# Work of a cycle's parameters and magnitude products moved between ScalarE, VectorE and GpSimd in a fused S4D and MLP-mixer kernel

## The chip, the cores and the metric

The kernel runs on one core of a Trainium2 chip. The time is that of the device in microseconds for one execution of the whole program; the profile gives one execution, with the busy intervals of each engine: PE (matmul, TensorE), PEld (its weight loads), DVE (VectorE), ACT (ScalarE), POOL (GpSimd) and SP (the queue from which most transfers are issued).

## What is computed

The input is one sequence of L = 2048 tokens and D = 448 channels. A vector c gives six modulation vectors by one matrix, w_mod. Two blocks follow, each behind a layer norm that is scaled and shifted:

```python
mod = (silu(c) @ w_mod).reshape(1, 6, 1, -1)
h = layernorm(x) * (1 + ca) + sa
x = x + ga * S4D(h)          # long convolution
h = layernorm(x) * (1 + cb) + sb
x = x + gb * MLP(layernorm(h))   # over the tokens, 2048 -> 1792 -> 2048, gelu

# S4D: the convolution's kernel, for each channel d and N = 256 complex terms n
dt = exp(log_dt);  A = -exp(log_A_real) + 1j * A_imag;  C = (C_real + 1j * C_imag) * dt
K[d, l] = 2 * Re(sum_n C[d, n] * exp(A[d, n] * dt[d] * l))       # l = 0 .. 2047
y = irfft(rfft(h, 4096) * rfft(K, 4096))[:2048] + h * D_skip
```

All is float32. The convolution is done by matmuls with tables of sines and cosines.

## The kernel before

The first half of the program makes K, the transforms of h and their product; the second, from about 366 us, is the layer norm and the two matmuls of the MLP with streamed weights.

**Steps and cycles.** K is made in 56 steps s; a step covers 16 channels' worth of terms (128 rows by 512 columns, twice). The power l is split into a small part and a large part, so that each step makes two factors, E and G, as magnitude times sine or cosine, and PE sums over n with 64 small matmuls (`st_kgen`). Steps go in cycles of 8. At a cycle's start `window(s)` takes the exponentials of all 8 steps in a row: PE makes the exponents (`st_exponents`), ACT the magnitudes (`st_exp`), and between them other work is slipped in for e = 0 to 7. Then come the 8 steps with sines (`st_phase` on PE, `st_step`), so that ACT changes its function table only twice or three times per cycle.

**A step.** ACT does two Abs (L651, L652) and four Sin (L653 to L656). GpSimd multiplies the two halves of G (L658, L659), VectorE the four quarters of E (L660, L661, then, behind `between()`, L663, L664). E needs m2 = magnitude times w, where w is a product of two columns; `st_mag2` (L637, L639) makes both on GpSimd. In cycle 0 the first two of these stand in the window at e = 4 and 5, the others in the steps, two steps ahead. There are three m2 buffers (`m2p`).

**Parameters.** Channels come in four sets of 128 rows (the last has 64, folded to 128 x 128). For set 0, `first_chain` computes at once what the exponent and phase matmuls need: log-magnitudes, phases, and the phase of C by an arctangent, each split into a high and a low part, which SP stores to DRAM (`pars`) and loads as `lex` and `lph`. For sets 1 to 3, `chain(q)` does the same as a Python generator that yields after each instruction. `more(n)` takes n steps of it and stops at "logs" (the chain waits until the window of its cycle does its logarithms and exponential on ACT in `logs`) and at "end". In the windows `WPACE[s // 8][e]` says how many steps are taken, in the sine steps `pace` (2 per step, in `between()`). `chain` starts with two Abs on ACT (L392, L393) and goes on with VectorE; only the splits (L382, L384) are on GpSimd, and only while `aside` is set, that is in the windows of cycles 1 to 3. Sets 1, 2 and 3 are due one after the other: set 1 must be in DRAM for step 16, set 2 for step 32, set 3 for step 48.

**Beside it.** `u_stats` (L500, L501, VectorE) takes the mean and variance of x, `u_norm` normalises it, `u_rows` (PE L531, VectorE L534) and `u_cols` (PE L563, then VectorE L570 or ACT L572) transform it, with transfers through DRAM between. `u_cols` needs a table s2 (`s2_load`, L548), loaded by SP four columns ahead. `modulation(k)` multiplies c by a 448 x 448 part of w_mod (PE L487); the parts 0 to 2 are loaded into `wm0` (`wm_load`, L323), a big tile that is used for yk only from step 8 on. The back of `wm0` holds the split parts of set 0 until SP has stored them. x is loaded in parts, four rows by SP and the rest by GpSimd's own queue (L298) at the start and behind steps 1 and 2.

**Order.** PE, ACT, VectorE and GpSimd run in the order in which the program writes their instructions; SP does so up to step 8, and is ordered by the scheduler after that. Each engine's queue is in order. A transfer is counted on one of eight completion slots in turn, and its issue waits for the transfer before it in that slot.

Of the kernel before, what the change touches and what calls it, by code (L numbers as in the profile page):

```python
# [11 lines left out]
F32 = mybir.dt.float32  # L12
F32R = mybir.dt.float32r
BF16 = mybir.dt.bfloat16
AF = mybir.ActivationFunctionType
# [205 lines left out]
def tile_adaln_s4d_mixer(ctx, tc, i, out):  # L221
# [20 lines left out]
    with ExitStack() as es:  # L242
# [24 lines left out]

        raws = {}

        def par_load(q, eng=nc.sync):  # L270
            n = min(P, D - P * q)
            raws[q] = {}
            for nm in ("A_C_real", "A_C_imag", "A_log_A_real", "A_A_imag"):
                raws[q][nm] = qp.tile([P, N], F32, tag=nm, name=nm, bufs=2)
                for k in range(P // n):
                    c = slice(k * (N * n // P), (k + 1) * (N * n // P))
                    eng.dma_start(raws[q][nm][n * k : n * k + n, 0 : N * n // P], i[nm][P * q : P * q + n, c])

        ldt_v = i["A_log_dt"]
        ldt0 = qp.tile([P, 1], F32, name="ldt0")  # L280
# [88 lines left out]
        def chain(q):  # L369


            n = min(P, D - P * q)
            f = N * n // P
            cr, ci, a, aim = (raws[q][nm][:, 0:f] for nm in ("A_C_real", "A_C_imag", "A_log_A_real", "A_A_imag"))
            xa, ya, s, t, u, ph, p64 = (
                qp.tile([P, N], F32, tag=nm, name=nm)[:, 0:f] for nm in ("xa", "ya", "s", "t", "u", "ph", "p64")
            )

            def split(src, places):
                hl = qp.tile([P, 2, N], F32R, tag="hl", name="hl", bufs=3)[:, :, 0:f]  # L380
                eng = G if aside else V
                eng.tensor_copy(hl[:, 0], src)  # L382
                yield
                eng.tensor_tensor(hl[:, 1], src, hl[:, 0].bitcast(F32), ALU.subtract)  # L384
                for k, v in places:
                    for m in range(P // n):
                        to = pars[q][v, k, 0:n, :, m * f : (m + 1) * f]
                        nc.sync.dma_start(to, hl[n * m : n * m + n].bitcast(F32))
                yield


            S.activation(xa, cr, AF.Abs, scale=0.5)  # L392
            S.activation(ya, ci, AF.Abs, scale=0.5)  # L393
            tt(s, xa, ya, ALU.add)
            yield
            tt(ya, ya, xa, ALU.subtract)
            yield
            ts(s, s, 2.0**-120, None, ALU.max)
            yield
            V.reciprocal(xa, s)  # L400
            yield
            tt(ya, ya, xa, ALU.mult)
            yield

            ts(t, s, 2.0**-40, 2.0**80, ALU.is_lt, ALU.mult)
            yield
            stt(s, t, 1.0, s, ALU.max, ALU.mult)
# [12 lines left out]
            yield from split(s, [(2, 1)])  # L420
            yield "exponents"

            ts(ph, aim, dt4[:, q : q + 1], None, ALU.mult)
            yield
            ts(u, ph, MAGIC, MAGIC, ALU.add, ALU.subtract)
            yield
            tt(ph, ph, u, ALU.subtract)
# [5 lines left out]
            tt(p64, ph, u, ALU.subtract)  # L433
# [17 lines left out]
            tt(xa, xa, u, ALU.subtract)  # L451
            yield
            yield from split(xa, [(2, 0)])
# [180 lines left out]
        def st_mag2(s):  # L634
            me = v32(mags[s][:, 0])
            w = wp.tile([P, GD], F32, tag="w", name="w")
            G.tensor_tensor(w[:, :, None], me[:, :, 31:32], me[:, :, 1:2], ALU.mult)  # L637
            m2 = m2p[s >= 32 and s % BATCH > 2].tile([P, GD, 32], F32, tag="m2", name="m2")
            G.tensor_tensor(m2, me, w[:, :, None].to_broadcast([P, GD, 32]), ALU.mult)  # L639
            m2s[s] = m2  # L640

# [177 lines left out]
        def first_chain():  # L819
# [19 lines left out]
            def direct(hl, tile, r, g):  # L839

                nc.sync.dma_start(tile[g][r : r + 32].bitcast(F32), hl[16 * g : 16 * g + 16])
# [8 lines left out]
            S.activation(dt[:, 0:1], ldt0, AF.Exp)  # L850

            S.activation(one, one, AF.Ln)
            par_load(1, nc.scalar)

            ts(sr, cr, 0.0, 0.5, ALU.is_ge, ALU.subtract)
            ts(si_, ci, 0.0, 0.5, ALU.is_ge, ALU.subtract)
# [8 lines left out]
            for g in range(4):  # L865
                direct(ha, lex, 0, g)
                if g < 3:
                    direct(ha, lex, 64, g)
            x_load(0, 4, G)
            S.activation(u, ya, AF.Square)  # L870
            S.activation(u, u, AF.Ln, bias=1.0)
# [38 lines left out]
            store(hc, (2, 0))  # L910

        first_chain()
        for g in (1, 2):
            load(g, False)
        x_load(4, 2)
# [48 lines left out]
        def window(s):  # L964
            if s:
                aside.append(True)
            angle()
            logs(s == 8)
            if s == 8:
                u_scale()  # L970
                u_norm(0)
                u_norm(1)

            if s == 8:
                modulation(0, 0, 1)
            if s == 0:
                st_exponents(s)
            for e in range(BATCH):
                st_exp(s + e)

                if e + 1 < BATCH:
                    st_exponents(s + e + 1)
                else:
                    st_phase(s)
                mellow()
                flush(dve)
                flush(act)
                if s == 8 and e == 0:
                    tt(mod[1], mod[1], mod[2], ALU.mult)
                if s < 32:  # L990
                    more(WPACE[s // 8][e])
                if s == 0 and e >= 4:
                    u_stats(e - 4)
                if s == 8 and e == 1:

                    G.tensor_tensor(mod[0], mod[0], mod[2], ALU.mult)
                if s and e < (2 if s <= 32 else 1):
                    st_kgen(s - (2 if s <= 32 else 1) + e)
                elif e == 5:
# [12 lines left out]

                if s >= 40 and e == 2:
                    piece(False)
                if s >= 40 and e == 4:
                    piece(pieces[0] < NP)
                if s == 0 and e in (4, 5):
                    st_mag2(e - 4)
                elif s and (e < 2 or s >= 32):
                    st_mag2(s + e)  # L1020
                if s == 8 and e == 0:
                    u_norm(e + 2)
                if s == 0 and e == 3:
                    for r in range(4):
                        dsk_copy(r)
            aside.clear()
            if s == 0:

                S.activation(one, one, AF.Sin)

        WPACE = [[1] * 8, [4, 4, 4, 4, 4, 4, 4, 1], [4, 4, 4, 4, 4, 4, 4, 1], [2] * 8]
        pace = [2] * 32
        tail = NHALF + 3
        for s in range(tail):
# [33 lines left out]
            else:  # L1070
# [6 lines left out]

                if s > 32 and s % BATCH:
                    st_kgen(s - 1)
                st_step(s, between)  # L1080
            flush(act)
            if s == NHALF:
# [3 lines left out]
            if s in (1, 2):  # L1086
                x_load(4 + 4 * s, 4, G)
            free = s > 7 and not st_s1(s % BATCH == BATCH - 1)
            if s + 2 < 32 and (s + 2) % BATCH > 1:
                st_mag2(s + 2)  # L1090

            if 3 < s < 8:
# [274 lines left out]
```

## Time and profile before

| | |
|---|---|
| three runs | 715.1, 719.54, 722.51 us; median 719.54 |
| the profiled execution | 720.75 us, its span 719.0 us |
| PE busy | 648.0 us, 90% of the span |
| DVE, ACT, POOL busy | 431.4, 453.1, 271.7 us |
| granted clock of PE, mean | 0.962 |
| transfers | 128.00 MB, 178 GB/s |

The stages of the first half lie thus in the profile: first exponentials 18.1 to 28.6 us, sines of cycle 0 to 65.4, exponentials of cycle 1 to 94.8, sines to 131.7, exponentials of cycle 2 to 153.6, sines to 187.3, exponentials of cycle 3 to 203.1, sines to 240.9, and three more cycles to about 366 us. A line of the groups gives line, engine, operation, output from input, count, then busy microseconds and mean nanoseconds, then idle time of the engine before them and what ended it. A line of the timeline or of the chain begins with the start and the duration in microseconds.

### The profile page before, as it was taken

The page shows a single profiled execution, that of the slowest core. Times are in us where ns is not written, and L with a number is a line of the kernel's source. Part 1 is how long each engine was busy: PE and PEld are TensorE (multiplying, and loading weights), DVE is VectorE, ACT ScalarE, POOL GpSimd, SP SyncE. Part 2 cuts the span into 40 slices and gives each one's busy share as a digit, 9 for nine tenths or more (in the row PEclk, how much of TensorE's full clock was granted, in tenths as well). Part 3 has the DMA queues.
Part 4 walks back from the last instruction along what each step waited for, and adds up shares of the span by engine and source line. Part 5 has one row for each costly group of instructions (what it writes and reads, how often), then busy time and mean ns, then how long its engine had stood idle before and what let it go on. Part 6 is the DMA issues. An engine that isn't in the chain of part 4 may idle for free.

```text
span 719.0 us, 18067 instructions
## 1 busy us (share of the span) xinstructions
PE 648.0 (90%) x7090; PEld 479.3 (67%) x7090; DVE 431.4 (60%) x821; ACT 453.1 (63%) x849; POOL 271.7 (38%) x341
## 2 busy tenths in 40 slices
PE   0777999879979879898999979999999999999997
PEld 0443444435535556575679936778999999999996
DVE  7668768758577567584855448778622263334441
ACT  4877487887986989999947649787522242222220
POOL 5395657548656866867745600000000000000000
PEclk9998758998999989999999999999999999999999
DMA  8494545556867656555459999984585436555540
GB/s 196 154 200 130 194 141 178 204 162 197 250 194 237 186 119 178 147 156 156 137 156 282 296 255 251 248 218 115 171 231 150 145 110 175 168 159 154 154 142 26
DMA packets 99395, 128.00 MB, mean 178 GB/s; under 512 B 13546, under 2 KB 80622, under 8 KB 99310
## 3 DMA queue, kind: packets, MB, share of 16 engines
q1 hardware_dynamic: 97726, 122.78, 60.3%
q0 software_dynamic: 1008, 3.54, 2.2%
q8 instruction: 56, 0.92, 0.6%
q10 hardware_dynamic: 576, 0.52, 0.3%
q14 instruction: 29, 0.24, 0.1%
HBM read 91.46 MB, written 34.87 MB: 176 GB/s over the span
## 4 chain that ended last, share of the span: by engine, by line
PE 65%; ACT 12%; DMA 9%; DVE 6%; issue 3%; POOL 3%; SPq 1%; DVEq 0%; ACTq 0%; POOLq 0%
PE acc L1191 6%; PE o L1333 6%; PE o L1335 6%; PE o L1334 6%; PE acc L1193 6%; PE acc L1192 6%; PE xe L610 6%; PE kg L685 4%; DMA wm<-in_w_mod_dram 4%; PE vv L794 3%; PE kx L778 3%; PE vv L795 3%; PE pu L563 2%; PE xg L610 2%; PE pm L487 2%
## 5 line engine op out<-in xcount | busy, mean ns | idle before, releaser
L206 ACT CAST whi<-w 128x896 fp32r<-128x896 f32 x64 | 59.8, 937 | 135.5 <-PE o L1334 84.8
L658 POOL TENSOR_TENSOR G<-mag,gs 128x512 f32<-128x512 f32 x56 | 72.0, 1286 | 69.3 <-ACT gs L654 69.1
L215 DVE TENSOR_TENSOR wlo<-w,whi 128x896 fp32r<-128x896 f32 x64 | 68.0, 1086 | 43.2 <-ACT whi L206 37.0
L1191 PE MATMUL acc<-h3h,whi 128*128 128x448 f32 x224 | 82.8, 370 | 0.8 <-ACT h3h L1242 0.8
L1192 PE MATMUL acc<-h3l,whi 128*128 128x448 f32 x224 | 80.9, 361 | 0.7 <-DVE h3l L1249 0.5
L1193 PE MATMUL acc<-h3h,wlo 128*128 128x448 f32 x224 | 81.3, 363 | 0.0
L1333 PE MATMUL o<-uh,whi 128*128 128x448 f32 x224 | 81.3, 363 | 0.0
L1335 PE MATMUL o<-uh,wlo 128*128 128x448 f32 x224 | 81.2, 362 | 0.0
L1334 PE MATMUL o<-ul,whi 128*128 128x448 f32 x224 | 80.6, 360 | 0.0
L610 PE MATMUL xg<-tab,lph 64*128 64x512 f32 x112 | 66.7, 597 | 12.6 <-DVE E L664 7.7
L685 PEld LDWEIGHTS kg<-E,G 128*32 128x32 f32 x3584 | 56.7, 115 | 31.1 <-issue 16.4
L610 PE MATMUL xe<-tab,lph 64*128 64x512 f32 x112 | 65.7, 592 | 9.3 <-ACT gs L655 7.6
L659 POOL TENSOR_TENSOR G<-mag,gs 128x512 f32<-128x512 f32 x56 | 71.8, 1282 | 0.0
L685 PE MATMUL kg<-E,G 128*32 128x64 f32 x3584 | 66.5, 229 | 3.4 <-ACT ks L699 2.0
L660 DVE TENSOR_TENSOR E<-m,xe 128x512 f32<-128x512 f32 x56 | 38.4, 686 | 46.6 <-ACT xe L653 30.3
L639 POOL TENSOR_TENSOR m<-mag,w 128x512 f32<-128x512 f32 x56 | 58.7, 1049 | 4.4
L1337 DVE SCALAR_TENSOR_TENSOR y<-o,b,mod 128x448 f32<-128x448 f32 x16 | 11.0, 685 | 80.2 <-PE o L1335 80.2
L1191 PEld LDWEIGHTS acc<-h3h,whi 128*128 128x128 f32 x224 | 42.0, 188 | 12.8 <-ACT h L1247 5.6
L786 DVE TENSOR_TENSOR z<-kx,u 128x448 f32<-128x448 f32 x48 | 28.4, 620 | 32.5 <-PE kx L778 32.5
L610 PE MATMUL xe<-tab,lex 64*128 64x512 f32 x56 | 29.8, 544 | 19.7 <-DMA lex<-wm 18.1
L651 ACT ACTIVATE ab<-xe 128x512 f32<-128x512 f32 x56 | 33.9, 606 | 17.4 <-PE xg L610 9.9
L1192 PEld LDWEIGHTS acc<-h3l,whi 128*128 128x128 f32 x224 | 41.9, 187 | 4.1 <-DVE h3l L1249 0.8
(221 smaller groups left out, 1514.7 us busy)
## 6 DMA issues: line engine op xcount, KB each, us to landing
w<-in_B_w_dram SPq DMA_DIRECT2D x64, 224.0 KB
w<-in_B_w_dram SPq DMA_DIRECT2D x32, 448.0 KB
u<-us_d SPq DMA_DIRECT2D x48, 224.0 KB
yu_d<-yt SPq DMA_DIRECT2D x16, 448.0 KB
yi<-yu_d SPq DMA_DIRECT2D x32, 224.0 KB
us_d<-uo SPq DMA_DIRECT2D x16, 448.0 KB
v_d<-vt SPq DMA_DIRECT2D x32, 224.0 KB
vt<-v_d SPq DMA_DIRECT2D x16, 448.0 KB
```

The lines of the kernel that those rows point to most:

```text
L206: self.nc.scalar.copy(hi, w)
L215: eng.tensor_tensor(lo, w, hi.bitcast(F32), ALU.subtract)
L610: T.matmul(out[k], lhs[r], rhs[r], start=start, stop=stop)
L658: G.tensor_tensor(Gt[:, 1], mg_, v32(sg), ALU.mult)
L659: G.tensor_tensor(Gt[:, 0], mg_, v32(cg_), ALU.mult)
L685: T.matmul(kgs[g][32 * q : 32 * q + 32, m], Gt[:, c, d], E[:, c, d], start=h == 0 and c == 0 and m == 0, stop=h == 1 and c == 1, skip_grou ...
L1191: nc.tensor.matmul(acc[f], hi[:, fs], h3h[:, r], start=r == 0, stop=False)
L1192: nc.tensor.matmul(acc[f], hi[:, fs], h3l[:, r], start=False, stop=False)
L1193: nc.tensor.matmul(acc[f], lo[:, fs], h3h[:, r], start=False, stop=r == 15)
L1333: nc.tensor.matmul(o, hi[:, ks], uh[kh][:, k], start=kh == 0 and k == 0, stop=False)
L1334: nc.tensor.matmul(o, hi[:, ks], ul[kh][:, k], start=False, stop=False)
L1335: nc.tensor.matmul(o, lo[:, ks], uh[kh][:, k], start=False, stop=kh == 1 and k == 6)
```

## The change

1. In cycle 0, six magnitude products (steps 0 to 5, at e = 2 to 7) are made in the window rather than two; three of them are put into the back of `wm0`, where the split parts of set 0 lay.
2. `chain(q)` puts all its tensor-scalar and tensor-tensor operations on GpSimd while `aside` is set, not the splits alone. An operation that VectorE does in one instruction with a scalar and a tensor takes two on GpSimd.
3. For set 1 the two Abs on ACT become two VectorE instructions each (times -0.5, then the larger of that and 0.5 times the input).
4. `WPACE` is changed, and `lead` takes 9, 5 and 3 further steps of the chain ahead of the first sine step of cycles 1, 2 and 3, when `aside` is no longer set, so on VectorE.
5. The loads of set 1 go from ACT's queue to SP's: two behind the first `lex` loads, two behind `first_chain`.

In the order of the instructions this puts 12 tensor-scalars and 7 two-input operations more into each of the windows of cycles 2 and 3 on GpSimd (128 x 256 and 128 x 128), 5 and 3 into that of cycle 1, and takes from it two splits there and one in the others. The Abs of sets 2 and 3 come some steps later, among the sines of cycle 1 and of cycle 2. Two operations of set 1 move into step 0. VectorE in steps 8 to 15 gets the end of chain 1 and all of chain 2's first part; in steps 24 to 31 it has no parameter work left.

```diff
-        def par_load(q, eng=nc.sync):
+        par_names = ("A_C_real", "A_C_imag", "A_log_A_real", "A_A_imag")
+
+        def par_load(q, names=par_names):
...
+            on = lambda: G if aside else V
+            tt = lambda *a: on().tensor_tensor(*a)
+            ts = lambda *a: on().tensor_scalar(*a)
+
+            def stt(to, a, c, b, op0, op1):
+
+                if aside:
+                    G.tensor_scalar(a, a, c, None, op0)
+                    G.tensor_tensor(to, a, b, op1)
+                else:
+                    V.scalar_tensor_tensor(to, a, c, b, op0, op1)
...
-            S.activation(xa, cr, AF.Abs, scale=0.5)
-            S.activation(ya, ci, AF.Abs, scale=0.5)
+            for to, src in (xa, cr), (ya, ci):
+                if q > 1:
+                    S.activation(to, src, AF.Abs, scale=0.5)
+                else:
+                    ts(to, src, -0.5, None, ALU.mult)
+                    yield
+                    V.scalar_tensor_tensor(to, src, 0.5, to, ALU.mult, ALU.max)
+                    yield
...
-            m2 = m2p[s >= 32 and s % BATCH > 2].tile([P, GD, 32], F32, tag="m2", name="m2")
+            if s in (3, 4, 5):
+                m2 = v32(wm0.rearrange("p k d -> p (k d)")[:, -512 * (s - 2) :][:, 0:512])
+            else:
+                m2 = m2p[s >= 32 and s % BATCH > 2].tile([P, GD, 32], F32, tag="m2", name="m2")
...
-            par_load(1, nc.scalar)
...
+            par_load(1, par_names[0:2])
             x_load(0, 4, G)
...
         first_chain()
+        par_load(1, par_names[2:4])
...
-                if s == 0 and e in (4, 5):
-                    st_mag2(e - 4)
+                if s == 0 and e > 1:
+                    st_mag2(e - 2)
...
-        WPACE = [[1] * 8, [4, 4, 4, 4, 4, 4, 4, 1], [4, 4, 4, 4, 4, 4, 4, 1], [2] * 8]
+        WPACE = [[0, 2, 2, 1, 1, 1, 1, 1], [2, 2, 2, 2, 2, 2, 1, 0], [3] * 8, [3] * 8]
+        lead = {8: 9, 16: 5, 24: 3}
...
+                more(lead.get(s, 0))
                 st_step(s, between)
...
-            if s + 2 < 32 and (s + 2) % BATCH > 1:
+            if s + 2 < 32 and (s + 2) % BATCH > 1 and s + 2 > 5:
                 st_mag2(s + 2)
```

More of the change, by code (lines that the diff above doesn't have):

```diff
@@ L268, in tile_adaln_s4d_mixer @@
         raws = {}
-        def par_load(q, eng=nc.sync):
+        par_names = ("A_C_real", "A_C_imag", "A_log_A_real", "A_A_imag")
+        def par_load(q, names=par_names):
             n = min(P, D - P * q)
-            raws[q] = {}
-            for nm in ("A_C_real", "A_C_imag", "A_log_A_real", "A_A_imag"):
+            raws.setdefault(q, {})
+            for nm in names:
                 raws[q][nm] = qp.tile([P, N], F32, tag=nm, name=nm, bufs=2)
@@ L276, in par_load @@
                     c = slice(k * (N * n // P), (k + 1) * (N * n // P))
-                    eng.dma_start(raws[q][nm][n * k : n * k + n, 0 : N * n // P], i[nm][P * q : P * q + n, c])
+                    nc.sync.dma_start(raws[q][nm][n * k : n * k + n, 0 : N * n // P], i[nm][P * q : P * q + n, c])
         ldt_v = i["A_log_dt"]
@@ L377, in chain @@
             )
+            on = lambda: G if aside else V
[7 more added lines that the diff above has]
+                    V.scalar_tensor_tensor(to, a, c, b, op0, op1)
             def split(src, places):
                 hl = qp.tile([P, 2, N], F32R, tag="hl", name="hl", bufs=3)[:, :, 0:f]
-                eng = G if aside else V
-                eng.tensor_copy(hl[:, 0], src)
+                on().tensor_copy(hl[:, 0], src)
                 yield
-                eng.tensor_tensor(hl[:, 1], src, hl[:, 0].bitcast(F32), ALU.subtract)
+                tt(hl[:, 1], src, hl[:, 0].bitcast(F32), ALU.subtract)
                 for k, v in places:
@@ L406, in chain @@
             yield
-            stt(s, t, 1.0, s, ALU.max, ALU.mult)
+            V.scalar_tensor_tensor(s, t, 1.0, s, ALU.max, ALU.mult)
             yield
```

## The prediction

> **What bounds the kernel now.** I read the busy table first, then the table of stretches cut at the ends of the stages (in the order span, PE, PEld, DVE, ACT and POOL busy, granted clock, DMA share, GB/s), then the chain that ended last inside each stretch.
>
> ```profile
> span 719.0 us, 18067 instructions
> PE 648.0 (90%) x7090; PEld 479.3 (67%) x7090; DVE 431.4 (60%) x821; ACT 453.1 (63%) x849; POOL 271.7 (38%) x341
> 28.62:65.42 36.80, 28.54 (x460) 15.93 (x457) 26.88 (x53) 27.59 (x55) 29.84 (x35) 0.91 0.72 163
> 65.42:94.81 29.39, 25.57 (x272) 10.65 (x273) 18.04 (x41) 17.51 (x36) 15.68 (x23) 0.75 0.59 197
> 94.81:131.74 36.93, 33.86 (x572) 16.95 (x572) 31.78 (x52) 32.92 (x62) 27.83 (x28) 0.78 0.48 156
> 131.74:153.57 21.83, 20.86 (x319) 10.21 (x319) 12.56 (x29) 15.51 (x32) 8.29 (x15) 1.00 0.48 177
> 187.30:203.08 15.78, 15.04 (x289) 7.96 (x290) 7.45 (x18) 13.76 (x29) 5.92 (x12) 1.00 0.77 225
> 203.08:240.90 37.82, 30.71 (x535) 16.69 (x535) 29.67 (x49) 29.91 (x60) 26.94 (x30) 0.95 0.65 207
> 40.88 19.11 DMA wm<-in_w_mod_dram
> 60.54 8.94 DMA wm<-in_w_mod_dram
> ```
>
> PE is 90% busy over the span, and the MLP behind 366 us is its own affair; this change ends before 250 us. The six rows that begin with two times are the sines of cycle 0, the exponentials of cycle 1 (65.42), its sines, the exponentials of cycles 2 and 3, and the sines of cycle 3. GpSimd is the busiest non-PE engine in the first of them (29.84 of 36.80 us), but the two chain rows say that the end of that stretch belongs to two loads of w_mod, 28 us of the chain; PE's modulation matmuls wait for the second until 69.5. In the second row the clock granted is 0.75, and DVE is busy 18.04 us.
>
> **The change, part by part.** The profiled execution took 720.75 us (span 719.0), the median of the three runs is 719.54; I sum against 720.75 and carry the result over, less 1.2.
>
> *Start.* The two Abs of set 1 leave ACT, and the four loads of set 1 leave ACT's queue for SP's.
>
> ```profile
> 14.70 0.79 SPq L841 DMA_DIRECT2D lex<-wm  x1
> 17.76 0.57 SPq L841 DMA_DIRECT2D lex<-wm  x1
> 21.05 0.41 ACT xa L392
> 21.46 0.30 ACT ya L393
> 33.13 0.69 DVE L663 TENSOR_TENSOR E<-mag,xg 128x512 f32<-128x512 f32 x1 [0.16 <-ACT xg L656]
> ```
>
> The Abs stand in the chain, between two of the first exponentials: 0.41 + 0.30 = 0.7 us go. The load that the second matmul waits for was issued at 17.76, and what stands before it ended at 15.5. SP now issues two 128 KB loads ahead of it (bound +1 us: two issues and 256 KB), while four such loads no longer occupy DMA engines and completion slots earlier (bound -2.3, from 17.76 back to 15.5). I take -1, between the ends, since the number of bytes ahead of it falls. Two operations of set 1 now fall into step 0 between E's halves on DVE, where E at 33.13 waited only 0.16 us: two operations of 0.3 to 0.4 us and possibly a hold; I take +1.0 (0 to +1.5). Net -0.7, bounds -3.0 to +1.8.
>
> *Six products earlier.* Four pairs w, m2 leave GpSimd's sines of cycle 0 for the exponentials.
>
> ```profile
> L639 POOL TENSOR_TENSOR m<-mag,w 128x512 f32<-128x512 f32 x39 | 40.9, 1048 | 3.1
> L637 POOL TENSOR_TENSOR w<-mag 128x16 f32<-128x16 f32 x39 | 10.2, 262 | 3.1 <-ACT mag L621 3.0
> 18.06:28.62 10.56, 9.09 (x22) 4.79 (x23) 8.28 (x23) 8.64 (x18) 3.31 (x6) 1.00 0.51 176
> 52.59 0.63 DVE L500 BATCH_NORM_STATS2 st<-xt 128x6 f32<-128x448 f32 x1 [3.69 <-DMA xt<-in_A_u_dram]
> ```
>
> 4 x (1.05 + 0.26) = 5.2 us, into a stretch where GpSimd has 10.56 - 3.31 = 7.2 us free; so the cover holds with 2 us to spare. What is late next is not GpSimd: DVE stands 3.69 us for x at step 4, and the w_mod load ends at 69.5 whatever GpSimd does. GpSimd issues that x load right after its products, so it goes out 1 to 3 us sooner, into queues that carry the same bytes. I take 0 (-3 to 0).
>
> *Exponentials of cycle 1.* Chain 1's operations leave DVE.
>
> ```profile
> 80.42 0.87 DVE ph L423
> 81.65 1.15 DVE ph L427
> 83.47 1.72 PE pu L531 x4
> 80.84 0.50 PE L610 MATMUL xe<-tab,lex 64*128 64x512 f32 x1
> 85.12 0.79 PE L610 MATMUL xe<-tab,lex 64*128 64x512 f32 x1
> 98.00:100.00 2.00, 2.00 (x64) 1.59 (x64) 2.00 (x5) 1.97 (x5) 1.64 (x2) 0.50 0.17 52
> 74.00:76.00 2.00, 2.00 (x72) 1.25 (x74) 0.00 (x0) 1.47 (x3) 1.92 (x5) 1.00 0.02 7
> ```
>
> DVE's parameter work (80.42 to 82.80) stands in the chain ahead of the evictions that PE's pu at 83.47 needs. That wait goes: 1.5 us. Right behind it the granted clock is 0.50, and the same matmul grows from 0.50 to 0.79 us; the stretch 83.47 to 94.81, 11.34 us, would be 11.34 x 0.50/0.79 = 7.2 us at full clock: 4.2 us less. I take both, 5.7, less 0.7 for other gaps: -5 (bounds -1.5 to -8, the latter if the steps behind profit too). A rule speaks for less: the Trainium skill, "TensorE: Matmul & The Clock Gate", Part 1, has the full clock back after about 3.4 us of sustained work. By it only 3.4 x (1 - 0.63) = 1.3 us would be won there; the row at 98 does not agree: PE is filled, and the clock, low since 83, is still 0.50.
>
> *GpSimd in the exponentials.* Cycle 1 gains five tensor-scalars and three two-input operations and loses two splits; cycles 2 and 3 gain twelve and seven and lose one split.
>
> ```profile
> L384 POOL TENSOR_TENSOR hl<-p,hl 128x256 fp32r<-128x256 f32 x2 | 1.5, 733 | 0.2
> L382 POOL CAST hl<-p 128x256 fp32r<-128x256 f32 x2 | 0.8, 396 | 1.6 <-DVE p L433 1.6
> L518 POOL TENSOR_SCALAR xt<-xt,rs,nm 128x448 f32<-128x448 f32 x6 | 5.1, 853 | 4.3 <-DVE nm L509 4.3
> L384 POOL TENSOR_TENSOR hl<-p,hl 128x128 fp32r<-128x128 f32 x1 | 0.5, 457 | 0.0
> 136.40 0.40 POOL L382 CAST hl<-A_log_A_real 128x256 fp32r<-128x256 f32 x1 [4.52 <-ACT A_log_A_real L464]
> 157.12 1.27 POOL L658 TENSOR_TENSOR G<-mag,gs 128x512 f32<-128x512 f32 x1 [6.40 <-ACT gs L654]
> ```
>
> No 128x256 tensor-scalar on GpSimd is shown: between the cast of that size (0.40) and the 128x448 one (0.85); I take 0.55, nearer the cast. Cycle 2: 8.29 - 1.13 + 7 x 0.73 + 12 x 0.55 = 18.9 us (17.1 to 22.5) in the 20.7 us from 136.40 to the first G at 157.12: it fits at my value, and is 1.8 us late at the upper end. Three DVE operations of some 0.4 us come after it and ahead of E: 0 (0 to +3.4). Cycle 1: 15.68 - 2.26 + 2.2 + 5 x 0.55 = 18.4 of 29.39: free. Cycle 3 at half the width, with the half-wide cast of 0.29 us in the fence on steps 24 to 31: 5.92 + 7 x 0.46 + 12 x (0.29 to 0.46), at most 14.6 of 15.78: fits. The nine operations "ahead of the first sine" in cycle 1 fill DVE's wait there.
>
> *Steps 8 to 15.* DVE now ends chain 1 here and does all of chain 2's first part: six operations more than before.
>
> ```profile
> L396 DVE TENSOR_TENSOR ya<-ya,xa 128x256 f32<-128x256 f32 x2 | 0.8, 420 | 0.0
> L427 DVE TENSOR_TENSOR ph<-ph,u 128x128 f32<-128x128 f32 x1 | 0.3, 293 | 0.0
> L451 DVE TENSOR_TENSOR xa<-xa,u 128x128 f32<-128x128 f32 x1 | 1.4, 1381 | 0.0
> ```
>
> 6 x 0.42 = 2.5 us, and the same kind of operation took 0.29 or 1.38 us depending on whether GpSimd was in a product, a hold of up to 1.09: 2.5 to 9.1 us against 36.93 - 31.78 = 5.15 us free. I take 0 (-3 to +3.9; below nothing since the reciprocal leaves the crowded steps 8 and 9). Two Abs move from PE-bound exponentials onto ACT's sines at cycles 1 and 2; by 0.41 and 0.30 at most 0.7 each, of which I take +0.6 in all (0 to +1.4).
>
> *Steps 24 to 31.* Chain 3 ends before the first sine.
>
> ```profile
> 191.45 0.29 POOL L382 CAST hl<-A_log_A_real 128x128 fp32r<-128x128 f32 x1 [3.14 <-ACT A_log_A_real L464]
> 209.13 0.41 POOL hl L384
> 209.75 0.35 SPq L388
> 212.15 4.12 DMA s<-in_S_dram
> 216.41 1.59 PE pu L563 x2
> ```
>
> SP is in order: the load s2 (212.15) stands behind a store that waits for GpSimd's split of p64, which waits behind two G products. In the changed order the last store ahead of that load is xa's. GpSimd begins at 191.45 and, with the 13.5 us that lie amid the estimates above, is through by 205; DVE's three operations of at most 0.3 us follow, so the store goes at about 206; two stores and two yi loads, as from 209.75 to 212.15, take 2.4, and s2 is issued at about 208 rather than 212.15: -4.2 (0 to -5). Its cover gone, PE's pu waits for yi and the uo buffers as in other steps.
>
> Sum: -0.7 + 0 - 5 + 0 + 0 + 0.6 - 4.2 = -9.3, to 711.4; beside the median 710.2. I write 711.
>
> **The rivals.**
> *The clock falls all the same,* from a gap that I don't see: part three is worth 1.5, the sum -5.8, time 714 beside the median. For it: the granted clock of three successive stretches is 0.91, 0.75 and 0.78, so that gaps are common. Inside this case lies that the clock, once fallen, comes back as early as behind the wait that ended at 69.5 (1.00 again from 74, 4.5 us): then 4.5 x 0.37 = 1.7 is what a kept clock is worth, part three 3.2, time 712; chance 0.04, since the stretch behind 83 us took over 16 us. It is the rule of the Trainium skill's page on the clock gate, named above.
> *The load s2 is late anyway,* because it then waits for yi or the uo stores in the same queue: the sum is -5.1, time 714.5.
> *More:* x and w_mod come sooner as GpSimd issues x earlier (-3), and the full clock lasts into step 8 (-3): time 704.
> *DVE and GpSimd stand in each other's way* (slower). Place: steps 8 to 15 and the end of cycle 2's exponentials. It decides from a mean hold of (5.15 - 2.5)/6 = 0.44 us, or from 0.70 us per GpSimd tensor-scalar. Price: +3.9, +3.4, the clock dropping after that gap as at 83 us (+4.2), Abs +0.6, chain 3's stores late as before (0), start -0.7, and -1.5 for the wait that goes: +9.9, so 729.5. For it: the held rows, and some 18 more instructions on GpSimd in cycles 2 and 3 each. In a sentence apart: the Trainium skill, "GPSIMD Engine Reference", 4.1 Engine selection, gives elementwise work to VectorE, with GpSimd about twice as slow on two inputs; 0.73 against 0.42 agrees, 1.7 times. Against it: DVE's E, yt and uo read PSUM and show no such holds, and GpSimd idles 6.40 us ahead of G.
> *It does nothing:* every win lies ahead of a load that ends when it did; 719.
>
> **How the numbers follow.** Forecast 0.42 (its own range 706 to 717), clock 0.17, s2 0.10, more 0.12, in each other's way 0.15, nothing 0.04. The runs span 715.1 to 722.51, so 1%, 7.2 us, is about what can be told. Below 712.3: all of "more" and two thirds of the forecast with some of the next two, 0.43. Above 726.7: most of the slower case, 0.13. Between: 0.44. Range 702 to 723: it leaves out the slower case and little else.
>
> **What would show it.** Right: no L392, L393 among ACT's first exponentials; pu's wait on yt in cycle 1 gone, and 1.00 as clock from 76 us to the sine table; s2's load within 3 us of the first sine of cycle 3. Wrong: G of step 16 released by GpSimd's own chain; DVE operations of 1.2 us and more in steps 8 to 15; the w_mod wait still ending at 69.5 or later; clock 0.5 behind 83 us.

## The result, and the profile after

The changed kernel takes 736.89 us (median of four runs, 736.59 to 740.83) beside 719.29 for the kernel before on the same chip: 1.0249 times, interval 1.0210 to 1.0288. It is slower, by 17.6 us; the forecast was 711, and the range ended at 723.

The first lines of the page of the changed kernel, the table of its stretches from the exponentials of cycle 1 on, without the exponentials of cycle 3, which last as long as before (span, PE, PEld, DVE, ACT, POOL busy, granted clock, DMA share, GB/s; cut at the ends of the stages as for the kernel before), and the groups of GpSimd's operations of 128 x 256:

```profile
span 739.0 us, 18080 instructions
PE 651.3 (88%) x7090; PEld 483.1 (65%) x7090; DVE 423.2 (57%) x795; ACT 453.1 (61%) x847; POOL 301.4 (41%) x381
```

```profile
61.40:97.02 35.62, 25.11 (x273) 11.31 (x275) 13.54 (x31) 16.75 (x33) 19.66 (x27) 0.71 0.51 161
97.02:136.33 39.31, 34.91 (x612) 17.82 (x616) 35.91 (x66) 33.68 (x65) 28.49 (x28) 0.74 0.48 161
136.33:160.88 24.55, 24.32 (x293) 11.92 (x283) 5.61 (x10) 15.10 (x29) 18.39 (x26) 0.79 0.30 114
160.88:203.83 42.95, 29.98 (x484) 15.61 (x488) 29.86 (x49) 30.03 (x61) 31.67 (x34) 0.84 0.65 186
219.45:258.47 39.02, 32.05 (x533) 16.96 (x534) 26.55 (x42) 30.09 (x59) 31.36 (x37) 0.87 0.69 219
```

```profile
L383 POOL TENSOR_SCALAR u<-ph 128x256 f32<-128x256 f32 x3 | 3.2, 1076 | 0.2
L383 POOL TENSOR_SCALAR s<-s,ldt 128x256 f32<-128x256 f32 x2 | 1.9, 929 | 0.1
L388 POOL TENSOR_SCALAR t<-t 128x256 f32<-128x256 f32 x2 | 1.7, 862 | 0.2
L389 POOL TENSOR_TENSOR s<-t,s 128x256 f32<-128x256 f32 x2 | 1.5, 729 | 0.2
```

The sines of cycle 0 end at 61.4 instead of 65.4: the start has won 4 us in this execution. Then it goes the other way. The exponentials of cycle 1 last 35.6 us instead of 29.4, the sines of cycle 2 43.0 instead of 33.7, the exponentials of cycle 2 and the sines of cycles 1 and 3 1 to 3 us more each. In none of these stretches is GpSimd or VectorE full: VectorE's busy time even fell in the row of 61.40 from 18.04 to 13.54. So the time is in waits, and in the exponentials of cycle 2, where PE is full (24.32 of 24.55 us), in the granted clock, 0.79 instead of 1.00. A tensor-scalar of GpSimd in these groups takes 0.86 to 1.08 us, more than the two-input operation of the same size (0.73); the prediction had 0.55.

**Cycle 1.** From the timeline of the changed kernel (start, duration, then the idle time before it and what ended it):

```profile
77.06 0.33 SPq L555 DMA_DIRECT2D yu_d<-yt  x1
81.56 0.73 POOL L382 TENSOR_TENSOR hl<-s,hl 128x256 fp32r<-128x256 f32 x1
82.31 0.32 SPq L401 DMA_DIRECT2D pars<-hl  x1
83.22 0.47 SPq L279 DMA_DIRECT2D A_A_imag<-in_A_A_imag_dram  x1
85.71 0.72 POOL L382 TENSOR_TENSOR hl<-ph,hl 128x256 fp32r<-128x256 f32 x1
86.46 0.32 SPq L401 DMA_DIRECT2D pars<-hl  x1
86.88 0.38 SPq L555 DMA_DIRECT2D yu_d<-yt  x1
89.88 1.16 DVE L553 TENSOR_TENSOR yt<-pu,mod 128x448 f32<-128x448 f32 x2 [7.48 <-DMA yu_d<-yt]
90.56 1.98 PE L745 MATMUL y<-wc,ks 64*64 64x64 f32 x62 [6.59 <-DVE yt L553]
92.47 0.79 PE L629 MATMUL xe<-tab,lex 64*128 64x512 f32 x1
```

SP issues nothing between the first yu_d (77.06) and the store of s, which goes the moment GpSimd has made its split (at 82.29, 81.56 + 0.73). Between that and the store of ph (split ready at 86.43, 85.71 + 0.72) it issues only a load of set 3's A_A_imag that overwrites what GpSimd has just read. Only then, at 86.88, comes the second yu_d, whose data VectorE had ready since 79.4. There are three yt buffers, so VectorE waits 7.48 us for that store, PE 6.59 us for VectorE, and behind the gap the clock is low (0.79 us for the matmul that takes 0.50). GpSimd itself is through 10.6 us before the first sine: the prediction's "free" was true of the engine and missed what stands behind its stores.

**Cycle 2.**

```profile
140.87 0.40 POOL L395 CAST hl<-A_log_A_real 128x256 fp32r<-128x256 f32 x1 [4.54 <-ACT A_log_A_real L483]
...
164.76 1.08 POOL L383 TENSOR_SCALAR u<-xa 128x256 f32<-128x256 f32 x1
165.87 1.48 DVE L382 TENSOR_TENSOR xa<-xa,u 128x256 f32<-128x256 f32 x1 [13.36 <-POOL u L383]
168.99 0.68 DVE L682 TENSOR_TENSOR E<-m,xe 128x512 f32<-128x512 f32 x1
169.10 0.31 SPq L401 DMA_DIRECT2D pars<-hl  x1
169.11 0.31 ACT L407 ACTIVATE xa<-A_C_real 128x128 f32<-128x128 f32 x1 [3.75 <-DVE hl L382]
169.59 0.68 DVE L683 SCALAR_TENSOR_TENSOR E<-mag,xe 128x512 f32<-128x512 f32 x1
170.38 0.76 PE L629 MATMUL xe<-tab,lph 64*128 64x512 f32 x1 [6.72 <-ACT mod L510]
171.86 11.79 SPq L573 DMA_DIRECT2D yi<-yu_d  x10
179.19 3.21 PE L582 MATMUL pu<-yi,s 128*128 128x448 f32 x4 [5.02 <-DMA yi<-yu_d]
```

GpSimd works through set 2 and two magnitude products without a pause from 140.87 to 165.84, 25 us, where 18.9 were forecast for the same work. VectorE has to finish the set and stands 13.36 us for it, in order, with E queued behind; SP has to store xa, in order, with the yi loads queued behind; PE stands 6.72 us for the one and 5.02 for the other. The profile puts the 6.72 us down to ACT's mod (L510); by the program's order they are E's, since the matmul writes one of the two xe buffers that E reads, the second quarter of E ended at 170.27, and the matmul began at 170.38. ACT is a third queue held by the same set: the two Abs of set 3 (L407) stand in it ahead of mod and of step 17's Abs, and overwrite the xa that set 2's last split still reads, so ACT stood 3.75 us.

**Cycle 3.** Set 3 ends the same way, at half the width:

```profile
225.24 1.34 DVE L382 TENSOR_TENSOR xa<-xa,u 128x128 f32<-128x128 f32 x1 [6.21 <-POOL u L383]
228.15 1.18 SPq L401 DMA_DIRECT2D pars<-hl  x2
230.73 0.59 SPq L567 DMA_DIRECT2D s<-in_S_dram  x1
```

The load s2 goes at 230.73, 11.3 us behind the first sine of its cycle (219.45), where it went 9.1 us behind it before and 4.9 were forecast.

### The profile page after: what moved, and what is told of

Read it like the earlier page. It is cut to its first block, busy times and chain, and to the rows that moved or that the text cites. A ratio compares the mean times of both kernels' runs of the same rounds, so it can differ in the third digit from the quotient of the medians.

```text
span 739.0 us, 18080 instructions
## 1 busy us (share of the span) xinstructions
PE 651.3 (88%) x7090; PEld 483.1 (65%) x7090; DVE 423.2 (57%) x795; ACT 453.1 (61%) x847; POOL 301.4 (41%) x381
## 4 chain that ended last, share of the span: by engine, by line
PE 58%; ACT 12%; POOL 9%; DMA 7%; DVE 7%; issue 5%; SPq 1%; POOLq 0%; DVEq 0%; ACTq 0%
PE acc L1216 6%; PE o L1359 6%; PE o L1358 6%; PE o L1360 6%; PE acc L1217 6%; PE acc L1218 6%; PE xe L629 5%; PE kg L707 4%; PE pu L582 2%; DMA si<-in_SK_dram 2%; PE kx L800 2%; PE vv L816 2%; PE xg L629 2%; PE vv L817 2%; ACT gs L674 2%
## 5 line engine op out<-in xcount | busy, mean ns | idle before, releaser
L707 PEld LDWEIGHTS kg<-E,G 128*32 128x32 f32 x3584 | 58.6, 118 | 30.8 <-issue 20.2
L707 PE MATMUL kg<-E,G 128*32 128x64 f32 x3584 | 68.5, 233 | 2.4 <-issue 1.8
L682 DVE TENSOR_TENSOR E<-m,xe 128x512 f32<-128x512 f32 x53 | 36.3, 686 | 38.6 <-ACT xe L675 26.6
L661 POOL TENSOR_TENSOR m<-mag,w 128x512 f32<-128x512 f32 x53 | 56.0, 1056 | 4.1
L673 ACT ACTIVATE ab<-xe 128x512 f32<-128x512 f32 x56 | 33.8, 603 | 30.7 <-PE xg L629 17.4
L629 PEld LDWEIGHTS xe<-tab,lph 64*128 64x128 f32 x112 | 23.5, 210 | 39.8 <-ACT gs L677 7.3
L808 DVE TENSOR_TENSOR z<-kx,u 128x448 f32<-128x448 f32 x48 | 28.4, 620 | 34.2 <-PE kx L800 34.1
L629 PE MATMUL xe<-tab,lex 64*128 64x512 f32 x56 | 29.4, 540 | 18.6 <-DMA lex<-wm 17.1
```

The source lines that it names most:

```text
L629: T.matmul(out[k], lhs[r], rhs[r], start=start, stop=stop)
L707: T.matmul(kgs[g][32 * q : 32 * q + 32, m], Gt[:, c, d], E[:, c, d], start=h == 0 and c == 0 and m == 0, stop=h == 1 and c == 1, skip_grou ...
```

## Experiments

The table gives, for every kernel's profiled execution, the length of the stages in us, cut on ACT's timeline at the first Abs of a cycle's steps and at the arctangent behind its last, with the median of its runs and the ratio to the kernel before. The last column ends at the first exponential of cycle 4, which has no arctangent ahead of it; the table above ends that stage 1.3 us earlier, where ACT loads its table of functions. The sines of steps 8 to 15 last 37.7 to 38.0 us in a_pace and pace_only and 40.4 to 40.5 in set2, set3 and set2_x, which also have all of set 1 on VectorE, at granted clocks of 0.87 to 0.91 and of 0.79, so I read nothing below 3 us there.

| kernel | exp 1 | sin 8-15 | exp 2 | sin 16-23 | exp 3 | sin 24-31 | median us | ratio (95%) |
|---|---|---|---|---|---|---|---|---|
| before | 29.4 | 36.9 | 21.8 | 33.7 | 15.8 | 39.1 | 719.29 | |
| changed | 35.7 | 39.2 | 24.7 | 42.8 | 15.8 | 40.3 | 736.89 | 1.0249 (1.0210-1.0288) |
| a_only | 31.7 | 35.3 | 21.8 | 33.8 | 15.8 | 40.2 | 717.88 | 0.9973 (0.9944-1.0002) |
| a_pace | 27.3 | 37.7 | 21.8 | 34.7 | 15.8 | 34.2 | 712.83 | 0.9918 (0.9887-0.9949) |
| pace_only | 25.2 | 38.0 | 21.8 | 34.8 | 16.1 | 34.2 | 716.45 | 0.9951 (0.9913-0.9988) |
| gp_only | 39.5 | 35.7 | 32.1 | 35.2 | 16.0 | 38.2 | 739.05 | 1.0291 (1.0249-1.0333) |
| half_ts | 34.3 | 39.4 | 23.5 | 38.3 | 15.7 | 40.2 | 731.26 | 1.0186 (1.0149-1.0222) |
| ts_on_v | 26.9 | 40.0 | 23.5 | 35.1 | 15.8 | 34.8 | 715.31 | 0.9939 (0.9906-0.9972) |
| g_store | 26.3 | 39.6 | 21.8 | 48.1 | 16.0 | 47.5 | 742.57 | 1.0354 (1.0279-1.0428) |
| half_g_store | 26.3 | 47.4 | 21.8 | 45.5 | 15.8 | 47.7 | 750.07 | 1.0418 (1.0348-1.0488) |
| set1 | 35.8 | 38.9 | 24.7 | 35.1 | 16.2 | 34.2 | 727.42 | 1.0124 (1.0066-1.0182) |
| set2 | 26.3 | 40.5 | 23.5 | 44.4 | 15.8 | 33.6 | 725.23 | 1.0076 (1.0037-1.0115) |
| set3 | 26.2 | 40.4 | 23.5 | 34.9 | 16.0 | 39.2 | 720.32 | 1.0010 (0.9980-1.0041) |
| set2_x | 24.9 | 40.4 | 23.5 | 39.2 | 15.8 | 34.0 | 720.98 | 1.0008 (0.9974-1.0041) |

**Which part of the change costs.** My theory was that GpSimd's chain loses and the rest wins a little; the rival was the new pacing with its operations ahead of the first sine. Three kernels divide the change into start (products, Abs, loads), chain on GpSimd, and pacing.

Start alone (a_only), and all but the chain on GpSimd (a_pace):

```diff
# a_only and a_pace, in the changed kernel
-            on = lambda: G if aside else V
+            on = lambda: V          # splits stay on GpSimd, as before
...
# a_only as well
-        WPACE = [[0, 2, 2, 1, 1, 1, 1, 1], [2, 2, 2, 2, 2, 2, 1, 0], [3] * 8, [3] * 8]
-        lead = {8: 9, 16: 5, 24: 3}
+        WPACE = [[0, 2, 2, 1, 1, 1, 1, 1], [4, 4, 4, 4, 4, 4, 4, 1], [4, 4, 4, 4, 4, 4, 4, 1], [2] * 8]
+        lead = {}
```

> The kernel before with the start of the change alone: six products under the exponentials of step 0, two Abs of set 1 on VectorE, the four loads of set 1 moved; sets 1 to 3 stay on VectorE with the pacing of before. Theory (the loss belongs to the chain on GpSimd, the early gain is real): first arctan 4 us earlier than before, 715.5 us (713 to 718). Rival (the early gain is hidden by what waits later): first arctan 4 us earlier, but 718.5 to 720.

> The changed kernel with the operations of sets 1 to 3 back on VectorE (splits on GpSimd as before), the new pacing and the operations ahead of a cycle's first sine kept. Theory (GpSimd's chain is the loss): 712 to 720 us. Rival (the pacing and the operations ahead of the first sine are the loss, whatever engine does them): 728 us or more.

The chain on GpSimd alone (gp_only), in the kernel before:

```diff
+            on = lambda: G if aside else V
+            tt = lambda *a: on().tensor_tensor(*a)
+            ts = lambda *a: on().tensor_scalar(*a)
...              # stt as in the change
```

> The kernel before with one edit: operations of sets 1 to 3 on GpSimd under the exponentials, at the pacing of before. Theory (GpSimd's chain is the loss, and the start hid 4 us of it): 737 to 745 us. Rival (the pacing is the loss): below 725 us.

And pacing alone, in the kernel before (pace_only): `WPACE` of cycles 1 to 3 and `lead` as in the changed kernel.

> The kernel before with the new pacing and the operations ahead of a cycle's first sine alone, all sets on VectorE; no products moved, no Abs, no loads. Theory (pacing frees the exponentials of cycle 1 of 2 to 4 us and lets the S2 loads of cycle 3 go ahead, 5 us; the start adds its 4 us beside it, of which 2 are given back in cycle 1): 713 to 716 us, sines 24 to 31 36 us or less. Rival (start and pacing need each other): 717 us or more.

The chain on GpSimd costs about 20 us by itself (739.05), and taking it out of the changed kernel gives 24 us back (736.89 to 712.83). The rival falls: the pacing is a small gain, 716.45 alone (0.1 to 0.9% below the kernel before, and 0.45 us above the range that I had written down), with sines 24 to 31 at 34.2. The start's gain is not told from none in time (the interval of a_only holds 1): its first arctangent comes 4.3 us sooner (61.15), but the exponentials of cycle 1 give 2.3 us back. The 4 us are not all the start's, either: without it that arctangent came at 62.12 in pace_only and 63.59 in gp_only, and with it at 65.24 in half_ts. a_pace, at 712.83 faster than both kernels (0.5 to 1.1% below the kernel before), is the version to keep; its stretches of cycles 1 and 3, and the load s2 with the wait of PE that it no longer causes:

```profile
62.39:89.65 27.26, 22.48 (x274) 10.69 (x274) 13.35 (x33) 16.77 (x33) 12.37 (x18) 0.81 0.62 189
199.58:233.78 34.20, 29.45 (x536) 15.54 (x536) 26.85 (x48) 31.07 (x60) 27.43 (x28) 1.00 0.72 232
```

```profile
205.53 0.59 SPq L565 DMA_DIRECT2D s<-in_S_dram  x1
208.03 2.59 PE L580 MATMUL pu<-yi,s 128*128 128x448 f32 x6 [1.32 <-ACT uo L589]
```

s2 goes 5.95 us behind the first sine (199.58), PE waits 1.32 us there instead of the 3.12 of the kernel before, whose row follows, and the clock stays at 1.00.

```profile
216.41 1.59 PE L563 MATMUL pu<-yi,s 128*128 128x448 f32 x2 [3.12 <-DMA s<-in_S_dram]
```

**Price or order.** Two things could make GpSimd's chain cost so much: that its operations are dear, or that what waits for it stands ahead of others in in-order queues. half_ts cuts the tensor-scalars of sets 1 and 2 to half the columns; ts_on_v takes them off GpSimd:

```diff
# half_ts (the sets keep their scratch tiles)
+            half = lambda v: v[:, 0 : v.shape[1] // 2] if aside and q < 3 else v
+            ts = lambda to, a, *b: on().tensor_scalar(half(to), half(a), *b)
...
+                    G.tensor_scalar(half(a), half(a), c, None, op0)
# ts_on_v
+            ts = lambda *a: V.tensor_scalar(*a)
...
+                    V.tensor_scalar(a, a, c, None, op0)
```

> The changed kernel with GpSimd's tensor-scalar operations of sets 1 and 2 on 128 of 256 columns, so that half the parameters of these sets are left stale; expected price of one 0.5 to 0.65 us instead of 0.85 to 1.08. Theory by price (the tensor-scalars alone make GpSimd late): chain of set 2 ends before the first G of cycle 2 needs it, 722 us or less. Rival by order (stores that wait for GpSimd stand ahead of other transfers in SP's queue, whatever one operation costs): 731 us or more; between, both.

> The changed kernel with the tensor-scalars of sets 1 to 3 on VectorE, and two-input operations and splits still on GpSimd. Theory by price: about 11 us of GpSimd's 25 us contiguous chain of set 2 go, its stores are 5 us earlier or more, 725 us or less. Rival (each result handed from one in-order engine to the other holds what is queued behind it on VectorE): 732 us or more.

The group of half_ts that stood at 1.08 us:

```profile
L384 POOL TENSOR_SCALAR u<-ph 128x128 f32<-128x128 f32 x5 | 3.3, 651 | 0.3
```

At 0.53 to 0.65 us each (one of them, of constants, 0.30), about the price that the prediction had taken, the kernel still takes 731.26: only 5.6 of the 24 us come back, and the exponentials of cycle 1 stay at 34.3. With the tensor-scalars gone altogether, 715.31, nearly all comes back, though each set still passes from engine to engine; so handing results over is not what costs here. Price matters, but nearly halving it is not enough.

g_store leaves GpSimd as late as it was and takes its stores out of SP's queue; half_g_store does both:

```diff
-                        nc.sync.dma_start(to, hl[n * m : n * m + n].bitcast(F32))
+                        (G if aside else nc.sync).dma_start(to, hl[n * m : n * m + n].bitcast(F32))
...
-                par_load(3)
+                par_load(3, par_names, G)
```

> The changed kernel; the stores of sets 1 to 3 that follow a GpSimd operation, and the eight loads of set 3, are issued by GpSimd instead of SyncE, so that nothing that waits for GpSimd stands ahead of yu_d and yi in SP's queue. GpSimd's work stays as late as it is. Theory by order: exponentials of cycle 1 30 us or less (35.7 in the changed kernel), sines 16 to 23 38 us or less (42.8), 727 us or less in all. Rival by time (GpSimd's own work ends too late, whoever issues its stores): 733 us or more.

> Both edits together: stores and set 3's loads issued by GpSimd, and GpSimd's tensor-scalars of sets 1 and 2 on 128 of 256 columns (half the parameters of these sets stale). Theory (price and order make up the loss in cycles 1 and 2): those cycles as long as with the operations on VectorE, 719 us or less, what is left being set 3's. Rival (a third cost, such as the operations of VectorE that take GpSimd's result and hold what is queued behind them): 724 us or more.

The timelines of the two around the yu_d stores, g_store first:

```profile
79.32 1.84 SPq L555 DMA_DIRECT2D yu_d<-yt  x2
82.69 1.16 DVE L553 TENSOR_TENSOR yt<-pu,mod 128x448 f32<-128x448 f32 x2 [0.37 <-PE pu L550]
88.88 0.64 POOL L401 DMA_DIRECT2D pars<-hl  x1 [0.30 <-POOL hl L382]
```

```profile
78.32 0.39 SPq L556 DMA_DIRECT2D yu_d<-yt  x1
87.57 0.50 SPq L620 DMA_DIRECT2D lex<-pars  x1
88.17 0.38 SPq L556 DMA_DIRECT2D yu_d<-yt  x1
93.28 0.62 DVE L554 TENSOR_TENSOR yt<-pu,mod 128x448 f32<-128x448 f32 x1 [10.09 <-DMA yu_d<-yt]
```

For cycle 1 the order is shown. In g_store GpSimd is through even later than in the changed kernel (its last store at 88.88), and yet the exponentials take 26.3 us, 9.4 less, since the yu_d stores go as they are ready. half_g_store missed: the scheduler, which orders SP, there put a load of lex that reads what GpSimd stores ahead of the third yu_d. The same wait came back (10.09 us) through a load instead of a store, and fell into the sines, 47.4 us. As a whole both were worse, and my forecasts for their totals wrong: GpSimd spends about 0.6 us on each of the stores (11.5 us for the 19 in g_store), within its chain, and cycles 2 and 3 end on that chain. In g_store VectorE got u at 160.5, 12.1 us behind the first sine of cycle 2, against 5.0 in the changed kernel.

**Set by set.** One set on GpSimd, the other two on VectorE but for their splits, which stay on GpSimd as in the kernel before:

```diff
-            on = lambda: G if aside else V
+            on = lambda: G if aside and q == 1 else V     # set1; set2 and set3 alike
```

> The changed kernel with sets 2 and 3 back on VectorE; set 1 alone on GpSimd. In SP's queue the store of set 1's s, the load of set 3's A_A_imag and the store of ph stand ahead of the second yu_d, as in the changed kernel. Theory by order: exponentials of cycle 1 34 us or more (35.7 in the changed kernel, 27.3 with all on VectorE, 26.3 with GpSimd as late but its stores in its own queue), 719 to 724 us in all. Rival (cycle 1's loss needs the other sets): 30 us or less, 716 us or less.

> The changed kernel with sets 1 and 3 back on VectorE; set 2 alone on GpSimd. Theory (GpSimd's chain of 25 us ends behind the first E of step 16, and the last store of the set stands ahead of the yi loads): exponentials of cycle 1 28 us or less, exponentials and sines of cycle 2 together 64 to 68 us (56.5 with all on VectorE, 67.5 in the changed kernel), 720 to 725 us in all. Rival (cycle 2 only inherits the lateness of cycle 1): 59 us or less together, 716 us or less. If the three sets add up, set 1, set 2 and set 3 alone lose together the 24 us that lie between 712.8 and 736.9.

> The changed kernel with the operations of sets 1 and 2 back on VectorE; set 3 alone on GpSimd. Theory (set 3's stores on SP hold the loads of cycle 3, also when cycle 2 is on time): sines 24 to 31 39 us or more against 34.2 with all on VectorE, 716 to 720 us in all. Rival (cycle 3 only inherits the lateness of cycle 2): sines 24 to 31 36 us or less, 715 us or less.

Each set lengthens its own cycle and leaves the later ones nearly as they are: set 1 the exponentials of cycle 1 to 35.8 (the 35.7 of the changed kernel), set 2 the sines of cycle 2 to 44.4, set 3 those of cycle 3 to 39.2. No cycle inherited its loss. They do not add up exactly: against a_pace, where the exponentials of cycle 4 end at 242.24, they end at 254.32, 254.13 and 251.01, so 12.1, 11.9 and 8.8 later, 32.8 together against 26.0 with all three (268.24). In each of the three, 4.1 to 4.5 us of it lie in steps 8 to 15 and the exponentials behind, and in the changed kernel 4.4. Counted once instead of three times, the sum is 12.1 + 11.9 + 8.8 - 4.1 - 4.5 - 4.5 + 4.4 = 24.1, near the 26.0. The totals, 727.42, 725.23 and 720.32, came out above the ranges that I had written down (they ended at 724, 725 and 720).

The rows say what the repeated part is. In a_pace and set3 PE, ACT, VectorE and GpSimd are given the same instructions up to cycle 3 (SP's order is the scheduler's), and the first Abs of step 14 comes 28.6 and 28.9 us behind that of step 8. From there to the end of the stage, a_pace first:

```profile
118.23:127.31 9.08, 7.70 (x159) 3.79 (x158) 9.08 (x20) 7.64 (x15) 5.94 (x5) 1.00 0.77 244
```

```profile
115.98:127.49 11.51, 10.10 (x193) 5.08 (x196) 10.18 (x22) 7.64 (x15) 5.91 (x5) 0.70 0.60 199
```

set2 has the same 11.51 us at 0.70, pace_only 9.07 at 1.00; in the exponentials behind, the clock is 0.93 in set2 and set3 and 1.00 in a_pace. PE's busy time is longer by 2.4 us, as much as the stretch. So in set2 and set3 this part is PE at a lower granted clock, and not a wait for GpSimd. What lowers the clock there in the one and not in the other is not shown.

**Set 2: which queue.** The loss of set 2 could lie in E held on VectorE or in the yi loads held on SP. Set 2's last store alone leaves SP's queue:

```diff
# in set2
-                        nc.sync.dma_start(to, hl[n * m : n * m + n].bitcast(F32))
+                        (G if q == 2 and places == [(2, 0)] else nc.sync).dma_start(to, hl[n * m : n * m + n].bitcast(F32))
```

> Set 2 alone on GpSimd as in the run before, but its last store, that of xa, is issued by GpSimd, behind the tail on VectorE and ahead of the first G of step 16; GpSimd's and VectorE's work end as late as they did (158 and 161 us), and that G starts up to 4 us later. Theory (xa's store ahead of the yi loads in SP's queue carries most of cycle 2's loss): first yi loads issued at 153 to 157 us instead of 164.2, exponentials and sines of cycle 2 together 60 to 64 us (67.8 in the run before, 56.5 with all on VectorE), 715 to 721 us in all. Rival (E, held on VectorE behind the tail, carries it): 66 us or more, 724 us or more.

From the timelines of set2 and of set2_x:

```profile
161.42 0.32 SPq L402 DMA_DIRECT2D pars<-hl  x1
162.51 0.28 DVE L382 TENSOR_TENSOR s<-xa,ya 128x128 f32<-128x128 f32 x1
164.19 11.11 SPq L574 DMA_DIRECT2D yi<-yu_d  x10
170.71 3.33 PE L583 MATMUL pu<-yi,s 128*128 128x448 f32 x4 [4.23 <-DMA yi<-yu_d]
```

```profile
158.01 13.46 SPq L574 DMA_DIRECT2D yi<-yu_d  x10
160.17 0.66 POOL L402 DMA_DIRECT2D pars<-hl  x1 [1.55 <-DVE hl L398]
160.98 2.54 DVE L382 TENSOR_TENSOR s<-xa,ya 128x128 f32<-128x128 f32 x1
161.16 0.76 PE L630 MATMUL xe<-tab,lph 64*128 64x512 f32 x1 [6.04 <-ACT mod L511]
```

The exponentials and sines of cycle 2 take 62.6 us instead of 67.8, and PE's 4.23 us for yi are gone: 5.2 of the 11.3 us above a_pace (56.5) go with that one edit. The loads went at 158.0, a little later than expected: they waited 2.1 us for the last yu_d store, and the yu_d stores still stand behind the store of p64. The wait of 6.04 us that is left is VectorE's, with E behind the set's tail. Not all of the 5.2 us need be the store's place in SP's queue. GpSimd waited 1.55 us for VectorE before it issued the store, and so multiplied G later; VectorE's last three operations of the set took 0.42, 0.29 and 0.43 us instead of 1.48, 1.24 and 0.43, and the first E came at 159.79 instead of 161.31. How the 5.2 us divide between the two is not shown.

## Why the prediction was wrong

**The step that failed is "GpSimd in the exponentials", "Cycle 1: 15.68 - 2.26 + 2.2 + 5 x 0.55 = 18.4 of 29.39: free".** The sum was nearly right (19.66 busy), the conclusion was not. It asked whether GpSimd would be through before the first sine, and did not follow the stores that this work feeds: they stand in SP's queue ahead of yu_d, and three yt buffers tie VectorE and PE to yu_d. Set 1 alone lengthens the stretch by 8.5 us (set1 against a_pace), and it stays long at the price of the prediction (half_ts, 34.3), and not at the measured price with the stores in another queue (g_store, 26.3).

Up to the first sine of cycle 4 the changed kernel is 17.6 us later in the profile (268.24 against 250.66), where 9.3 us sooner was forecast. Of these 26.9 us the exponentials of cycle 1 make 11.4, cycle 2 makes 11.9, the sines of cycle 3 make 5.4 and steps 8 to 15 make 2.3. Off go the 3.4 us that the start gave beyond the forecast and the 0.6 us that the forecast had for the moved Abs.

**The second term, cycle 2, was mis-sized.** Twelve tensor-scalars at 0.55 were taken; by the timeline they are one of 0.40 and eleven of 0.85 to 1.08, 11.1 us instead of 6.6, and with the gaps between instructions the chain takes 25.0 us instead of 18.9. The row of 0.85 for 128 x 448 that served as the upper bound was a multiplication with an addition; of that pair alone, the chain has one, at 0.40. Also, "three DVE operations ... ahead of E: 0 (0 to +3.4)" left out, as in cycle 1, what SP holds behind the store of their result: moving that store alone was worth 5.2 us in set 2. And the two Abs of set 3, taken with those of set 2 at +0.6 us in all by their own length, made ACT stand 3.75 us behind the set's tail (4.97 in set2, none in a_pace).

**Steps 24 to 31, -4.2,** had the right mechanism, the load s2 behind set 3's stores, and a wrong time for GpSimd's end: 13.5 us were counted from its start, and it took from 207.83, by the chain that begins as late behind the stage's start as before, until 225.2, 17.4 us, as tensor-scalars of 128 x 128 took 0.30 to 0.65 us where 0.29 to 0.46 had been taken. On VectorE with the new pacing the same edit brought 4.9 us (39.1 to 34.2).

**Exponentials of cycle 1, -5,** has a gain of that kind where the order allows it, but not its size and not clearly its cause: with set 1 on GpSimd and nothing of it in SP's queue 3.1 us (29.4 to 26.3), with the chain on VectorE 2.1 to 4.2 (a_pace, pace_only). The gain is as large with the operations still on VectorE, taken 2 instead of 4 behind each exponential, so that they leave VectorE is not shown to bring any of it. The clock did not stay full in them (0.81 in a_pace, 0.93 in pace_only). In the changed kernel the gap came back larger, and the matmul stood at 0.79 behind it, which was on the list of what would show the step wrong.

**Start, -0.7, and six products, 0:** both within what was measured; a_only's 0.9973 with its interval up to 1.0002 is no more than they say. In the changed kernel's profile the wait for w_mod ended at 67.5, not 69.5 as the prediction had it, and the arctangent came 4 us sooner; in a_only 2.3 us of that were given back in the exponentials of cycle 1.

**Steps 8 to 15, 0 (-3 to +3.9):** 2.3 us more, inside the range. Two of the end of set 1's operations were held there (1.25 and 1.24 us, at 102.21 and 106.24), as the prediction's list of signs against it had it, and two more in step 16 (1.48 above, and the cast behind it at 1.24).

**The rivals.** "DVE and GpSimd stand in each other's way" named the direction, one of the places (cycle 2) and, from the time that GpSimd has, the price from which it would come, 0.70 us per operation; eleven of the twelve were measured at 0.85 to 1.08. Its mechanism was only part of it: at 0.53 to 0.65, below that point, half_ts was still slower than the kernel before by 1.5 to 2.2%. Its price, 9.9 us, lacked cycle 1's 8.5 us and set 3's. What was forecast, 711, is close to what the change gives with its chain left on VectorE, 712.8; that is another kernel, its parts differ from the forecast's (2.1 us instead of 5 in the exponentials of cycle 1, 4.9 instead of 4.2 in steps 24 to 31), and the nearness is luck.

The rule weighed there, from the Trainium skill, "GPSIMD Engine Reference", 4.1 Engine selection, has GpSimd about twice as slow as VectorE on two inputs and roughly at line rate on one. The trace agrees on the first (0.73 to 0.42) and on the second only for casts and the one tensor-scalar of constants, 0.40 each: the other tensor-scalars, with one input, took 0.85 to 1.08 us where VectorE took 0.29 to 0.35 in a_pace.

```profile
80.57 0.35 DVE L383 TENSOR_SCALAR s<-s,ldt 128x256 f32<-128x256 f32 x1
83.97 0.29 DVE L383 TENSOR_SCALAR u<-ph 128x256 f32<-128x256 f32 x1
```

## What to carry to other kernels

When work moves to an engine that has time, follow what its results feed: a store that becomes ready later holds everything behind it in its in-order queue, and the cost is found at the buffers that those transfers free, here 7.5 us on VectorE in a stretch where GpSimd was idle for 10 us at the end. Price an operation by a row of the same pair of operations, and give each term its own time budget, from when the chain can start to when the next user in any queue needs it. And try the parts one by one: the pacing in this change was worth keeping, and was hidden by the part that was not.

## What the hardware showed that I had not expected

- On GpSimd a tensor-scalar of 128 x 256 took 0.40 us as a multiplication with an addition of constants, 0.86 as a multiplication alone, 0.93 with a scalar for each row added, and 1.08 as an addition with a subtraction or a comparison with a subtraction; the two-input operation took 0.73.
- VectorE's operations on SBUF were held while GpSimd multiplied: the same operation of 128 x 128 took 0.28 us in set2 and 2.54 in set2_x, where two G products (1.28 us each) ran beside it.
- Issuing a transfer occupied GpSimd about 0.6 us in g_store, 11.5 us for 19 stores.
- The granted clock had a mean of 0.70 over 11.5 us in set3 and stayed at 1.00 over the like stretch in a_pace, behind the same instructions of PE, ACT, VectorE and GpSimd.
